# Row sums inverted before the transpose of k and q, on 32 partitions of 28 numbers

## The chip, the cores and the metric

One core of a Trainium2 chip runs the kernel. The metric is the device time of one execution in microseconds (us). Five engines work side by side: TensorE (PE; its weight loads are listed apart as PEld), VectorE (DVE), ScalarE (ACT), GpSimd (POOL) and SyncE (SP). SP does no arithmetic here, it only issues transfers (DMAs); POOL issues transfers too. Each engine takes its instructions in the order of its own queue, and an instruction that waits holds back everything behind it in that queue.

## The reference

Softcapped attention over 4 batches of 12 heads (448 rows, head size 64, float32), then a two-layer MLP with a squared ReLU on its output (1792 tokens, 768 to 2048 to 768):

```python
def _attn_ref(q, k, v, cap):
    scale = 1.0 / np.sqrt(q.shape[-1])
    scores = scale * np.matmul(q, k.transpose(0, 1, 3, 2))
    scores = cap * np.tanh(scores / cap)
    scores = scores - np.max(scores, axis=-1, keepdims=True)
    attn = np.exp(scores)
    attn = attn / (np.sum(attn, axis=-1, keepdims=True) + 1e-09)
    return np.matmul(attn, v)

def _moe_ref(x, w_in, w_out):
    h = np.maximum(x @ w_in, 0.0)
    return h * h @ w_out
```

## The kernel before

The 48 heads are taken two at a time, as 24 pairs. The loop `for n in range(NP + 1)` (lines 535 to 586) is a software pipeline with several pairs in flight; one turn of it is called a pass here. The order of the instructions on PE, ACT, DVE, POOL and SP is written out by hand (`manual_schedule`), so the order of the source lines is the order of each queue. Pass n holds:

- On PE the scores of pair n (line 366, with half scores of two pairs at line 374 in even passes), and then, for pair n-1, the products of the probabilities with v (lines 408 and 424, into `pa`) and the row sums (lines 411 and 417, into `pb`). `pa` and `pb` have one PSUM buffer each: the first value matmul of a pass (line 408) has to wait until the pair before was copied out of them, the sums by `take_sums` (line 434, `es`) and the values by `evac` (line 429, `e`).
- On ACT tanh and exp of pair n (lines 384 and 392).
- On DVE in this order: `add_p3(n-1)` (line 399), `turn_kq(n+2)` (line 359, the transpose of k and q), `invert(n-2)` (lines 441 and 442), a piece of the decoding of `w_in`, the copy in `take_sums(n-1)` (line 434), `add_p(n)` (line 396), `normalise(n-3)` (lines 457, 460, 461) and `evac(n-1)` (line 429).
- On SP: the loads of q for pair n+3 and a part of n+4 (line 321, `load_part`; a pair is four parts of 56 KB, and passes 3 to 6 load five parts), the write of the inverted sums (line 444), from pass 4 on now and then a load of raw `w_in` (line 264, 384 KB), and the two transfers that bring the sums into `cmp` (line 437).
- On POOL: the two copies of the inverted sums of pair n-3 (`spread`, line 452), the loads of v (line 346) and the loads of k (line 321).

A pair's row sums take this way: the copy at line 434 brings them into SBUF; two transfers lay them out as `cmp` (112 partitions of 8 numbers); `invert` adds 1e-9 and takes the reciprocal on DVE; SP writes them to `rd` in DRAM; POOL reads them back over 64 partitions each as `rb`; `normalise` multiplies the values by them. In pass n, `cmp` of pair n-1 is sent, pair n-2 is inverted, and pair n-3 is spread and normalised.

k and q have three raw buffers (`kqn`). A load for pair n+3 goes where pair n was, whose transpose was two passes earlier. After pass 24 the MLP follows: the products with `w_in` (line 299) and with `w_out` (line 738).

Of the kernel before, what the change touches and what calls it, by code (L numbers as in the profile page):

```python
# [10 lines left out]
F32 = mybir.dt.float32  # L11
# [5 lines left out]
ALU = mybir.AluOpType  # L17
# [171 lines left out]
def tile_softcap_attention_mlp(ctx, tc, q, k, v, cap, w_in, w_out, out):  # L189
    nc = tc.nc  # L190
    B, H, S, D = q.shape
    NT, DM = out.shape
    DFF = w_in.shape[1]
    P = 128
    NS = S // D
    NT32 = S // 32
    HS = S // 2
# [38 lines left out]
    guard = const.tile([P, 1], F32, name="guard")  # L236
# [3 lines left out]
    ep = actx.enter_context(tc.tile_pool(name="ep", bufs=2))  # L240
# [76 lines left out]
    def load_part(n, i, a, queue):  # L317
        b, j = divmod(n, NPAIR)
        h, w = divmod(a, 2)
        x = (k, q)[i][b, 2 * j + h, :, 32 * w:32 * w + 32].rearrange("(t r) e -> r t e", r=32)  # L320
        queue.dma_start(out=kqn[n % NKQ][32 * a:32 * a + 32, i], in_=x)  # L321
# [19 lines left out]
    def load_v(n):  # L341
        b, j = divmod(n, NPAIR)
        x = v[b, 2 * j:2 * j + 2].rearrange("h (t r) d -> (h t) r d", r=D)
        for i in range(2):
            r, at = (bottom, 0) if (n + i) % 2 else (top, n % 2)
            nc.gpsimd.dma_start(out=vn[n % NKV][r, at:at + NS], in_=x[i::2].rearrange("t r d -> r t d"))
# [5 lines left out]
    kqs, ps, probs, adds, pvs, es, rds = {}, {}, {}, {}, {}, {}, {}  # L352


    def turn_kq(n, parts=1):
        kqs[n] = qp.tile([P, 2 * S], F32, tag="kq", name="kq")
        src, w = kqn[n % NKQ].rearrange("p i t e -> p (i t e)"), 2 * S // parts
        for i in range(parts):
            done = nc.vector.transpose(out=kqs[n][:, i * w:(i + 1) * w], in_=src[:, i * w:(i + 1) * w])  # L359
            last.setdefault("turn", done)  # L360

    def scores(n, u):
        sc = ps_s.tile([P, 2, 512], F32, tag="s", name="sc")
        kt, qt = kqs[n][:, :S], kqs[n][:, S:]
        for h, r in enumerate((top, bottom)):
            nc.tensor.matmul(out=sc[:, h, :S], lhsT=kt[r, keys(n, h, u)], rhs=qt[r], start=True, stop=True)  # L366
        probs[n, u] = sc
# [10 lines left out]
    def tanh(n, u):  # L378
        if u in (1, 3):
            c = 2 if u == 3 and n % 2 else 4  # L380
            ps[n, u // 3] = pp.tile([P, c, S], F32, tag=f"p{c}{u}", name="p", bufs=2 if c == 4 else 1)
        at = 2 * (u in (2, 0))
        p = ps[n, int(u not in (1, 2))][:, at:at + 2]
        nc.scalar.activation(out=p, in_=probs[n, u][:, :, :S], func=ACTF.Tanh, scale=qks)  # L384
        if u:
            probs[n, u] = p
        else:
            probs[n, 0], probs[n + 1, 0] = p[:, 0], p[:, 1]

    def exp(n, i):  # L390
        p = ps.pop((n, i))
        nc.scalar.activation(out=p, in_=p, func=ACTF.Exp, scale=cap_sb)  # L392
# [5 lines left out]
    def add_p3(n):  # L398
        nc.vector.tensor_add(out=adds[n], in0=adds[n], in1=probs[n, 3])
# [13 lines left out]
    def sums(n):  # L413
        a = adds.pop(n)
        for i in range(4):
            h, c = 1 - i // 2, slice(i % 2 * HS, (i % 2 + 1) * HS)
            nc.tensor.matmul(out=pvs[n, 1][32 * i:32 * i + 32, c], lhsT=ones[:, :32], rhs=a[:, h, c],  # L417
                             start=False, stop=True, tile_position=(0, 32 * i))
# [8 lines left out]
    def evac(n):  # L427
        es[n] = ep.tile([P, S], F32, tag="e", name="e", bufs=NE)
        nc.vector.tensor_copy(out=es[n], in_=pvs.pop((n, 0)))  # L429


    def take_sums(n):
        e = ep.tile([P, S], F32, tag="es", name="es", bufs=1)
        nc.vector.tensor_copy(out=e, in_=pvs.pop((n, 1)))
        rds[n] = ep.tile([P - 16, 8], F32, tag="cmp", name="cmp", bufs=NE)
        for c in range(2):
            nc.sync.dma_start(out=rds[n][c * 56:c * 56 + 56], in_=e[32 * c:P:64, c * HS:(c + 1) * HS])

    def invert(n):
        cmp = rds[n]  # L440
        nc.vector.tensor_scalar(out=cmp, in0=cmp, scalar1=guard[:P - 16], scalar2=None, op0=ALU.add)
        nc.vector.reciprocal(out=cmp, in_=cmp)
        rd = dram.tile([2, 2, HS], F32, tag="rd", name="rd")
        nc.sync.dma_start(out=rd.rearrange("c i (o e) -> (c i o) e", e=8), in_=cmp)
        rds[n] = rd


    def spread(n):
        rd = rds[n]
        rds[n] = ep.tile([P, S], F32, tag="rb", name="rb", bufs=2)  # L450
        for h, r in enumerate((top, bottom)):
            last["dma"] = nc.gpsimd.dma_start(out=rds[n][r].rearrange("p (c q) -> p c q", c=2), in_=rd[:, 1 - h].partition_broadcast(D))  # L452
# [34 lines left out]
    def prepare_cap():  # L487

        nc.vector.tensor_scalar_mul(ncap, cap_sb, -1.0)
        nc.vector.tensor_tensor(out=ncap, in0=ncap, in1=cap_sb, op=ALU.min)  # L490
        nc.vector.tensor_scalar(out=far, in0=ncap[0:1], scalar1=-CAP_MAX, scalar2=None, op0=ALU.is_lt)

        nc.scalar.activation(out=guard, in_=ncap, func=ACTF.Exp)

    def early_work():

        halves = [(f, o) for f in range(NEARLY + NW2) for o in range(0, DM, HO)]
        raw = fetch_w(scr, *halves[0], True, 2)
        yield
        for i, (f, o) in enumerate(halves):  # L500
            while f == NEARLY and not tail:
                yield
            if o == 0:
                hi, lo = hold_win(f, *((wpool, EARLY) if f < NEARLY else (qp, LATE)))
            coming = []
            if i + 1 < len(halves):
                wanted.append((coming, halves[i + 1]))
                if tail:
                    fetch_wanted()
            yield from decode_f64(nc, scr, raw, hi[:, o:o + HO], lo[:, o:o + HO], HO, NSCR,  # L510
                                  alone=lambda: not tail)
            raw = coming and coming[0]
            if o:
                decoded.append(f)
# [6 lines left out]
    decoded, tail, wanted = [], [], []  # L521
    decoding = early_work()
    NE = 2
    AHEAD = 1, 0
    START, DEEP = 4, 3

    def decode(count):
        for _ in range(count):
            next(decoding, None)

    def unit(f, b):
        hps[b, f] = ps_s.tile([P, 2, 512], F32, tag="s", name="hps")[:, 0, :S]
        mlp1_part(b, f, 0, 3 * KDM)

    for n in range(NP + 1):
        on, prep, old = n < NP, n + 1 < NP, n > 0

        if on:
            for u in (1, 2, 3):
                scores(n, u)  # L540
            tanh(n, 1)
            tanh(n, 2)
            exp(n, 0)
            tanh(n, 3)
        if n >= 3:
            spread(n - 3)
        if prep:
            load_v(n + 1)
        if n == 0:
            prepare_cap()  # L550
        if old:
            add_p3(n - 1)
        if 0 < n < NP - 2:
            turn_kq(2 if n == 1 else n + 2)
        upto = [min(4 * (m + 4) + min(4, max(0, m + 1 - DEEP)), 4 * NP) for m in (n - 1, n)]
        for i, queue in enumerate((nc.gpsimd, nc.sync)):
            for at in range(*upto):
                load_part(at // 4, i, at % 4, queue)
        if n == 1:
            nc.vector.tensor_scalar_mul(guard, guard, 1e-9)  # L560
        if n >= 2:
            invert(n - 2)
        if n >= START:
            decode(1 if n < NP - 2 else n - NP + 4)
        if n == NP:
            unit(0, 0)
        if old:
            pv_half(n - 1)
        if on and n % 2 == 0:
            half_scores(n)  # L570
            tanh(n, 0)
        if on:
            exp(n, 1)
        if old:
            sums(n - 1)
            take_sums(n - 1)
            fetch_wanted()
            pv(n - 1)
        if on:
            add_p(n)  # L580
        if n == 1:
            turn_kq(3)
        if n >= 3:
            normalise(n - 3)
        if old:
            evac(n - 1)
# [3 lines left out]
    units = [(f, b) for f in (0, 1) for b in range(B - 1)] + [(f, B - 1) for f in (0, 1)]  # L590
    units += [(f, b) for f in range(2, NEARLY) for b in range(B)] + [(NEARLY, b) for b in AHEAD]
    for i, (f, b) in enumerate(units):
# [90 lines left out]
    for f in range(NEARLY, NF):  # L683
# [19 lines left out]
        for b in reversed(range(B)):  # L703
            if f == NEARLY and b in AHEAD:
                continue
# [5 lines left out]
    with ExitStack() as mctx:  # L711
# [132 lines left out]
        for z in range(-6, N + 1):  # L844
# [9 lines left out]
            if 0 <= z + 2 < N:  # L854
                m, i = PRODUCTS[z + 2]
                ops[m, i] = operand(raws[m, i])
            if 0 <= z < N:
                weights(z)
                m, i = PRODUCTS[z]
# [39 lines left out]
```

## Time and profile before

| | us |
|---|---|
| median of 3 runs | 616.8 (616.15 to 618.32) |
| the profiled execution | 617.65 |
| its span from first to last instruction | 616.0 |
| PE busy | 602.5 (98%) |
| DVE busy | 484.6 (79%) |
| ACT busy | 336.1 (55%) |
| POOL busy | 125.6 (20%) |

The span is what the profile shows of one execution; what lies around it is 1.65 us. A busy PE is modelled from the starts of its matmuls. Shares over the whole span mix three stages: attention (to about 171 us), the first product of the MLP (to about 371 us) and the second. In the rows below a line such as L441 is line 441 of the kernel before. Idle time stands in brackets with the one that ended it by semaphore order; where the engine named had long been done, a transfer ended it.

### The profile page before, as it was taken

The numbers are of one execution on the slowest core, as the hardware profiler recorded it, in microseconds if no ns is written. First come the engines' busy times: TensorE is split into PE (matmuls) and PEld (weight loads), VectorE is DVE, ScalarE is ACT, GpSimd is POOL, SyncE is SP. The second block draws the span as 40 slices with busy tenths as digits, with TensorE's granted clock in tenths as the row PEclk, the third lists the DMA queues.
The fourth block names the chain that finished last, engine by engine and source line by source line (L and its number), as shares of the span: only waits on it lengthen the run. The fifth ranks groups of instructions, "written<-read, shape, count | busy, mean of one in ns | idle before, by whom it ended". The sixth has DMA issues, their size and how long they took to land.

```text
span 616.0 us, 9630 instructions
## 1 busy us (share of the span) xinstructions
PE 602.5 (98%) x3412; PEld 481.5 (78%) x3412; DVE 484.6 (79%) x840; ACT 336.1 (55%) x410; POOL 125.6 (20%) x197
## 2 busy tenths in 40 slices
PE   7998999999999999999999999999999999999997
PEld 4333333333369998999999999999999999999997
DVE  2778999999889663888999999834799998666752
ACT  5998899999933232555565555535334542222220
POOL 8678877686220000000000000000000000000000
PEclk9999999999999999999999999999999999999999
DMA  9999666774335433466657787689599807666611
GB/s 133 119 164 170 146 133 141 156 150 106 92 97 168 132 118 125 160 201 208 191 175 209 245 250 246 225 243 351 146 282 294 210 2 196 165 166 176 176 38 42
DMA packets 151671, 103.90 MB, mean 169 GB/s; under 512 B 58209, under 2 KB 142433, under 8 KB 151617
## 3 DMA queue, kind: packets, MB, share of 16 engines
q1 hardware_dynamic: 142432, 86.55, 52.4%
q0 software_dynamic: 7648, 16.41, 12.1%
q8 instruction: 28, 0.46, 0.3%
q10 hardware_dynamic: 1536, 0.27, 0.3%
q14 instruction: 27, 0.21, 0.1%
HBM read 79.69 MB, written 23.42 MB: 167 GB/s over the span
## 4 chain that ended last, share of the span: by engine, by line
PE 80%; DMA 9%; DVE 4%; POOL 2%; issue 2%; ACT 1%; SPq 0%; ACTq 0%; POOLq 0%; DVEq 0%
PE hps L299 32%; PE po L738 31%; PE pa L424 7%; PE sc L366 6%; DMA kqn<-in_k_dram 4%; PE pa L408 2%; DMA a<-g_dram 2%; PE pb L417 1%; POOL kqn L321 1%; DMA g_dram<-r 1%; PE sc L374 1%; DMA vn<-in_v_dram 1%; DMA rd<-cmp 1%; DMA rb<-rd 1%; DVE s L72 1%
## 5 line engine op out<-in xcount | busy, mean ns | idle before, releaser
L299 PE MATMUL hps<-xs,kq 128*128 128x448 f32 x864 | 173.2, 362 | 0.6 <-ACT r L303 0.6
L299 PEld LDWEIGHTS hps<-xs,kq 128*128 128x128 f32 x864 | 161.9, 187 | 11.8 <-ACT r L303 1.0
L738 PE MATMUL po<-th,gl 128*128 128x384 f32 x392 | 131.8, 336 | 0.6 <-DVE gl L728 0.6
L738 PE MATMUL po<-th,gh 128*128 128x384 f32 x392 | 131.8, 336 | 0.0
L738 PE MATMUL po<-tl,gh 128*128 128x384 f32 x392 | 131.7, 336 | 0.0
L727 ACT CAST gh<-a 128x1024 fp32r<-128x1024 f32 x49 | 51.6, 1053 | 110.8 <-PE po L738 103.4
L384 ACT ACTIVATE p<-sc,qks 128x896 f32<-128x896 f32 x84 | 80.4, 996 | 11.7 <-PE sc L366 11.5
L728 DVE TENSOR_TENSOR gl<-a,gh 128x1024 fp32r<-128x1024 f32 x49 | 59.9, 1223 | 28.6 <-ACT gh L727 28.5
L392 ACT ACTIVATE p<-p,cap_sb 128x1792 f32<-128x1792 f32 (+1 forms) x48 | 76.9, 1603 | 1.5
L303 ACT ACTIVATE r<-hps 128x448 f32<-128x448 f32 x64 | 34.8, 544 | 78.5 <-PE hps L299 78.5
L738 PEld LDWEIGHTS po<-th,gl 128*128 128x128 f32 x392 | 73.7, 188 | 1.0 <-DVE gl L728 1.0
L738 PEld LDWEIGHTS po<-th,gh 128*128 128x128 f32 x392 | 73.7, 188 | 0.3 <-ACT gh L727 0.3
L738 PEld LDWEIGHTS po<-tl,gh 128*128 128x128 f32 x392 | 73.7, 188 | 0.0
L366 PE MATMUL sc<-kq 64*128 64x448 f32 x288 | 60.6, 553 | 0.5 <-DVE kq L359 0.5
L424 PE MATMUL pa<-p,vn 128*64 128x448 f32 x288 | 59.4, 548 | 0.0
L321 POOL DMA_DIRECT2D kqn<-in_k_dram x92 | 58.8, 646 | 2.0 <-DMA kqn<-in_k_dram 1.0
L299 PE MATMUL hps<-xs,whi 128*128 128x448 f32 x192 | 54.1, 363 | 0.0
L366 PEld LDWEIGHTS sc<-kq 64*128 64x128 f32 x288 | 25.8, 186 | 34.4 <-issue 18.7
L424 PEld LDWEIGHTS pa<-p,vn 128*64 128x64 f32 x288 | 18.5, 136 | 30.9 <-issue 30.5
L452 POOL DMA_DIRECT2D rb<-rd x48 | 29.1, 611 | 54.6 <-DVE e L429 10.1
L299 PEld LDWEIGHTS hps<-xs,whi 128*128 128x128 f32 x192 | 35.8, 187 | 3.6 <-issue 1.4
L751 DVE TENSOR_TENSOR osb<-s,po 128x384 f32<-128x384 f32 x27 | 14.9, 553 | 27.4 <-PE po L738 27.3
(80 smaller groups left out, 746.8 us busy)
## 6 DMA issues: line engine op xcount, KB each, us to landing
a<-g_dram SPq DMA_DIRECT2D x56, 512.0 KB
g_dram<-r SPq DMA_DIRECT2D x64, 224.0 KB
wraw<-in_moe_w_in_dram SPq DMA_DIRECT2D x32, 384.0 KB
wraw<-in_moe_w_out_dram SPq DMA_DIRECT2D x32, 384.0 KB
vn<-in_v_dram POOLq DMA_DIRECT2D x48, 112.0 KB, 4.0
rb<-rd POOLq DMA_DIRECT2D x48, 112.0 KB, 3.6
kqn<-in_q_dram SPq DMA_DIRECT2D x93, 56.0 KB
kqn<-in_k_dram POOLq DMA_DIRECT2D x92, 56.0 KB, 3.7
```

The costliest lines, as they stand in the source:

```text
L299: nc.tensor.matmul(out=ps, lhsT=w[:, c * P:(c + 1) * P], rhs=x[b, c], start=(n == 0), stop=(n == 3 * KDM - 1))
L303: nc.scalar.activation(out=r, in_=ps, func=ACTF.Relu)
L321: queue.dma_start(out=kqn[n % NKQ][32 * a:32 * a + 32, i], in_=x)
L366: nc.tensor.matmul(out=sc[:, h, :S], lhsT=kt[r, keys(n, h, u)], rhs=qt[r], start=True, stop=True)
L384: nc.scalar.activation(out=p, in_=probs[n, u][:, :, :S], func=ACTF.Tanh, scale=qks)
L392: nc.scalar.activation(out=p, in_=p, func=ACTF.Exp, scale=cap_sb)
L424: nc.tensor.matmul(out=pvs[n, 0][r], lhsT=vn[n % NKV][:, v_slot(n, h, u)], rhs=p[:, h], start=False, stop=(u == NU - 1))
L452: last["dma"] = nc.gpsimd.dma_start(out=rds[n][r].rearrange("p (c q) -> p c q", c=2), in_=rd[:, 1 - h].partition_broadcast(D))
L727: last["act"] = nc.scalar.copy(out=hi, in_=x)
L728: last["dve"] = nc.vector.tensor_sub(out=lo, in0=x, in1=f32(hi))
L738: last["mm"] = nc.tensor.matmul(out=po, lhsT=w[:, c], rhs=m[:, cols], start=(c == 0 and i == 0), stop=(c == HF - 1 and i == 2))
L751: nc.vector.tensor_tensor(out=osb, in0=x, in1=y, op=op)
```

## The change

The inversion of the row sums stands ahead of `turn_kq` and of the loads of k and q in each pass, and no longer behind them. `cmp` becomes 32 partitions of 28 numbers: the two transfers into it move 16 runs of 112 bytes each where they moved 56 runs of 32 bytes, and the write to `rd` moves 32 runs of 112 bytes where it moved 112 of 32.

```diff
 def take_sums(n):
     e = ep.tile([P, S], F32, tag="es", name="es", bufs=1)
     nc.vector.tensor_copy(out=e, in_=pvs.pop((n, 1)))
-    rds[n] = ep.tile([P - 16, 8], F32, tag="cmp", name="cmp", bufs=NE)
+    rds[n] = ep.tile([NC, HB], F32, tag="cmp", name="cmp", bufs=NE)
     for c in range(2):
-        nc.sync.dma_start(out=rds[n][c * 56:c * 56 + 56], in_=e[32 * c:P:64, c * HS:(c + 1) * HS])
+        nc.sync.dma_start(out=rds[n][c * (NC // 2):(c + 1) * (NC // 2)], in_=e[32 * c:P:64, c * HS:(c + 1) * HS])

 def invert(n):
     cmp = rds[n]
-    nc.vector.tensor_scalar(out=cmp, in0=cmp, scalar1=guard[:P - 16], scalar2=None, op0=ALU.add)
+    nc.vector.tensor_scalar(out=cmp, in0=cmp, scalar1=guard[:NC], scalar2=None, op0=ALU.add)
     nc.vector.reciprocal(out=cmp, in_=cmp)
     rd = dram.tile([2, 2, HS], F32, tag="rd", name="rd")
-    nc.sync.dma_start(out=rd.rearrange("c i (o e) -> (c i o) e", e=8), in_=cmp)
+    nc.sync.dma_start(out=rd.rearrange("c i (o e) -> (c i o) e", e=HB), in_=cmp)
     rds[n] = rd
...
 NE = 2
+HB = 28
+NC = 2 * S // HB
...
     if old:
         add_p3(n - 1)
+    if n >= 2:
+        invert(n - 2)
     if 0 < n < NP - 2:
         turn_kq(2 if n == 1 else n + 2)
     upto = [min(4 * (m + 4) + min(4, max(0, m + 1 - DEEP)), 4 * NP) for m in (n - 1, n)]
...
             load_part(at // 4, i, at % 4, queue)
     if n == 1:
         nc.vector.tensor_scalar_mul(guard, guard, 1e-9)
-    if n >= 2:
-        invert(n - 2)
     if n >= START:
         decode(1 if n < NP - 2 else n - NP + 4)
```

## Rows read from the trace of the kernel before

**Rows 1.** Stretches of the span: us, busy time by engine, granted clock, DMA share, GB/s

```profile
25.00:29.00 4.00, 4.00 (x24) 1.63 (x20) 3.79 (x7) 3.97 (x5) 0.29 (x1) 1.00 0.28 40
29.00:41.00 12.00, 12.00 (x84) 4.13 (x82) 8.82 (x16) 11.77 (x11) 10.37 (x17) 1.00 1.12 153
...
67.00:171.00 104.00, 103.99 (x692) 36.79 (x692) 98.98 (x171) 99.46 (x87) 72.32 (x112) 1.00 0.58 129
...
241.00:371.00 130.00, 130.00 (x650) 121.86 (x651) 111.80 (x267) 71.75 (x133) 0.00 (x0) 1.00 0.66 206
```

**Rows 2.** Timeline of TensorE, first value matmul of passes 4, 5 and 8: start, length

```profile
35.77 0.59 PE L408 MATMUL pa<-p,vn 64*64 64x448 f32 x2
...
44.30 0.59 PE L408 MATMUL pa<-p,vn 64*64 64x448 f32 x2 [1.42 <-ACT p L384]
...
67.01 0.59 PE L408 MATMUL pa<-p,vn 64*64 64x448 f32 x2 [1.15 <-DVE e L429]
```

**Rows 3.** Chain that ended last, first value matmul of pass 10: start, length, what

```profile
80.41 0.52 PE pa L408 x2
```

**Rows 4.** Timeline of VectorE, passes 2 to 7; in brackets idle time before and releaser

```profile
22.16 1.07 DVE L399 TENSOR_TENSOR add<-add,p 128x896 f32<-128x896 f32 x1
25.01 1.11 DVE L359 STREAM_TRANSPOSE kq<-kqn 128x896 f32<-128x896 f32 x1 [1.78 <-DMA kqn<-in_k_dram]
...
35.63 1.08 DVE L399 TENSOR_TENSOR add<-add,p 128x896 f32<-128x896 f32 x1
38.99 1.11 DVE L359 STREAM_TRANSPOSE kq<-kqn 128x896 f32<-128x896 f32 x1 [2.29 <-DMA kqn<-in_q_dram]
...
44.11 1.08 DVE L399 TENSOR_TENSOR add<-add,p 128x896 f32<-128x896 f32 x1
...
46.85 0.50 DVE L441 TENSOR_SCALAR cmp<-cmp,guard 112x8 f32<-112x8 f32 x1 [0.64 <-DMA cmp<-es]
...
57.12 0.63 DVE L457 TENSOR_TENSOR rb<-e,rb 128x448 f32<-128x448 f32 x1 [0.77 <-DMA rb<-rd]
...
64.71 0.63 DVE L457 TENSOR_TENSOR rb<-e,rb 128x448 f32<-128x448 f32 x1 [0.93 <-DMA rb<-rd]
```

**Rows 5.** Timeline of the SyncE queue, passes 2 to 4, issues merged

```profile
19.85 2.98 SPq L321 DMA_DIRECT2D kqn<-in_q_dram  x4
26.50 0.33 SPq L444 DMA_DIRECT2D rd<-cmp  x1
...
28.11 2.51 SPq L321 DMA_DIRECT2D kqn<-in_q_dram  x5
31.15 0.32 SPq L444 DMA_DIRECT2D rd<-cmp  x1
...
32.76 3.03 SPq L321 DMA_DIRECT2D kqn<-in_q_dram  x5
40.58 0.32 SPq L444 DMA_DIRECT2D rd<-cmp  x1
40.95 0.43 SPq L264 DMA_DIRECT2D wraw<-in_moe_w_in_dram  x1
41.43 1.08 SPq L437 DMA_DIRECT2D cmp<-es  x2
```

**Rows 6.** Timeline of GpSimd, pass 3: the copies of the inverted sums

```profile
28.71 1.21 POOL L452 DMA_DIRECT2D rb<-rd  x2 [3.85 <-DMA rd<-cmp]
```

**Rows 7.** Chain that ended last: two transfers of the sums

```profile
27.56 1.63 DMA cmp<-es
...
31.15 4.68 DMA rd<-cmp
```

**Rows 8.** All instructions by line: mean ns of one, idle before

```profile
L441 DVE TENSOR_SCALAR cmp<-cmp,guard 112x8 f32<-112x8 f32 x24 | 6.2, 258 | 1.7 <-DMA cmp<-es 1.7
...
L442 DVE RECIPROCAL cmp<-cmp 112x8 f32<-112x8 f32 x24 | 4.9, 203 | 0.8
...
L483 DVE RECIPROCAL qks<-cap_sb 128x1 f32<-128x1 f32 x1 | 0.2, 163 | 0.3 <-DMA cap_sb<-in_cap_dram 0.3
```

## Prediction

> **What bounds the kernel now.** I read the stretches first, because shares over the whole span mix three stages. From 67 us to the end of attention PE stands still for 0.01 us of 104, and in the first product of the MLP for nothing; the granted clock is 1.00, the higher of the two levels, 2.4 GHz [rows 1]. What the change does to a pass after 67 us is therefore hidden behind PE, as long as DVE keeps up: DVE has 5.02 us to spare in those 104 us, 0.32 us for each of their 15.5 passes of 6.70 us [rows 1 to 3].
>
> Before 67 us PE is not the bound. The timeline of PE shows where passes begin: from pass 4 at 35.77 to pass 8 at 67.01 they take 31.24 us, 7.81 us each [rows 2]. Two passes of a full PE take 80.41 - 67.01 = 13.40 us [rows 2, 3], so four need 26.80. The difference, 4.44 us, is all that a change in this stage can give. PE waits there for buffers that DVE empties late, and the timeline of DVE says why DVE is late: 2.29 us at the transpose of pass 4, 0.64 us for `cmp` in pass 5, 0.77 and 0.93 us for `rb` in passes 6 and 7 [rows 4]; a fifth wait, 0.48 us for `rb` in pass 5, I leave out. Behind these waits stand transfers. The DMA engines are busy beyond one queue's worth from 29 to 41 us (1.12), yet nearly idle from 25 to 29 (0.28) [rows 1]: POOL waits 3.85 us there for the inverted sums of pair 0 [rows 6], and with it all loads of v and k behind that instruction.
>
> **The change part by part.** *The inversion moves ahead of the transpose.* In pass 2 the transpose waits 1.78 us for k and takes 1.11 us, and the write of `rd` goes out at 26.50 [rows 4, 5]. Put behind the addition that ends at 22.16 + 1.07 = 23.2, the inversion waits only for `cmp`, which I put at 23.6; it takes some 0.5 us, so `rd` leaves at 24.1, 2.4 us earlier, and POOL starts at 26.3 where it started at 28.71 [rows 6]. Loads of v and k follow 2.4 us earlier, into the hole from 25 to 29. The 2.29 us at the transpose of pass 4 have q as their releaser in the profile [rows 4], but k, which lies behind `rb` in POOL's queue, is as late. With k 2.4 us earlier and q landing in time (next part) they go: the addition of pass 4 ends at 36.7, the inversion at 37.4, and the transpose follows there and not at 38.99, 1.6 us earlier. DVE reaches the addition of pass 5 at some 42.2 and not 44.11 [rows 4].
>
> *SP's queue is turned round, and this gives most of that back.* Before, SP issued `cmp` first, then the q loads, and then waited for the next inversion: at 41.43 `cmp`, at 32.76 the five q loads of pass 4, at 40.58 `rd` [rows 5]. The loads were issued while SP waited. Now they stand behind `rd`, and `cmp` of the next pair stands behind them. In pass 2 four loads move from 19.85 to some 24.4, in pass 3 five move from 28.11 to some 30.5 [rows 5]. Their data are wanted one pass later (at some 30.1 and 37.4), 3 to 4 us after the last is issued, so I cost the loads themselves at nothing; if that cover fails, the transpose waits for the rest. What costs is `cmp`. With nothing in front a transfer of the sums takes 1.63 us; behind five q loads it takes 4.68 [rows 7]. The first was a transfer into `cmp`, the second a write to `rd`; the nearest rows there are.
>
> This makes a closed ring of waits in each pass: `rd` is issued (0.32 us), five q loads (2.51 to 3.03, taken as 2.65), two transfers into `cmp` (1.08) [rows 5], they land (call it x, in place of 1.63 to 4.68), the inversion runs (0.53) and the next `rd` is issued. The sum is 4.58 + x. DVE's own way from `rd` to that copy of sums (transpose 1.11, a piece of decoding, a copy) is shorter than the q loads. At x = 2.12 the ring takes 6.70 us, the period of a full PE; at x = 3.23 it takes 7.81, the period before; above that the change loses.
>
> Pass by pass: in pass 5 `cmp` lies behind five q loads and 384 KB of raw `w_in`. Before, only `w_in` was close ahead of it: issued from 41.43, it landed at 46.8 [rows 4, 5]. The bytes queued ahead of it since 32.76 are the same in both, so I put its landing at 46.3, while the inversion wants it at 43.2. DVE stands 3.1 us, and with the transpose then still to do, all but 0.2 us of the lead is gone. From there POOL has no work until `rd` of this pass lands, so SP's transfers find the engines free: in passes 6 and 7 I take x = 2.5, and the waits of 0.77 and 0.93 us for `rb` [rows 4] fall away, since `rd` leaves before the transpose (1.11 us). Lead 0.7 us after pass 6, 1.2 after pass 7. That is 30.0 us for the four passes, 7.5 each, a mean x of 2.9. From pass 7 on only four parts are loaded, some 0.5 us less, so the ring needs 4.1 + x and stays below 6.70 up to x = 2.6; the engines are at 0.58 there [rows 1].
>
> A rule of the Trainium skill bears on this. The rows show 1.63 us with nothing ahead and 4.68 us behind five loads [rows 7]. "DMA: Bandwidth & Descriptors", section "Queues, rings and completion order", says that each DMA engine consumes a queue's descriptors in ring order and that a semaphore update lands only after the earlier writes of that engine; by that, `cmp` always pays for the loads now ahead of it, in an idle stage too, and the sum would be that of the third rival below, 619.5. The two rows agree with the order; whether the loads ahead take long enough is x.
>
> *Fewer and longer runs.* 16 runs in place of 56, 32 in place of 112. Bounds: nothing, and the 1.63 us of a whole small transfer [rows 7]. Both stay one small transfer, so I take 0.1 us, inside x.
>
> *Longer instructions on DVE.* The reciprocal took 203 ns on 8 numbers a partition and 163 on one [rows 8]: 5.7 ns a number, so 20 more add 0.11 us. Bounds: nothing, and 203 x 28/8, 0.51 us more. The addition of 1e-9 (258 ns [rows 8]) I bound the same way, by nothing and by 0.65 us more; the rows don't part its start from its numbers, the reciprocal's slope would give it 0.11, and I take 0.02. Together 0.13 us a pass (0.22 with that slope), under the 0.32 us that DVE has to spare, which is what hides it. "VectorE: DVE Perf Modes", section "First, the fixed hardware budget", gives the reciprocal a repeat count of 8 on its divider; at that page's 0.96 GHz this is 8.3 ns a number and an estimate of 0.17 us a pass, still under the spare time.
>
> **Sum.** Profiled time 617.65 (span 616.0 and 1.65 around it), less 1.2: 616.4. The median of the runs is 616.8, 0.85 below the profiled execution, so I expect 615.6. The lead reaches the end because PE hardly stops after 67 us [rows 1].
>
> **The rivals.** *Full gain* (x at 2.1 or less from pass 4 on): DVE stays ahead and PE never waits: up to 4.44 us, half to all of it likely, about 3.4, so 613.4. For it: 1.63 us with free engines, and the hole filled. Against it: 1.12 of DMA share until pass 5 [rows 1].
> *Nothing* (x near 3.2): the waits at `rb` become waits at `cmp` of the same length; 616.8. It is also what comes if the transpose was late by q and not by k.
> *Slower by the ring* (x = 3.9): `cmp` stays behind the q loads, the inversion blocks DVE ahead of the transpose, 8.48 us a pass, +2.7 over four passes: 619.5. It decides from x = 3.23; for it stands 4.68, against it that POOL goes idle while SP loads.
> *Slower by DVE*: at the upper bounds (0.51 + 0.65 - 0.32 = 0.84 us over 15.5 passes) +13; with the reciprocal's alone 0.19 x 15.5, +2.9: 619.7.
>
> **How the numbers follow.** Forecast 0.45 (its own range 614.3 to 617), full gain 0.22, nothing 0.17, slower by the ring 0.12, slower by DVE 0.04. A measurement tells about 0.3% from no change, 1.85 us: below 614.95 is faster, above 618.65 slower. Of the forecast 0.14 lies below, 0.29 within, 0.02 above. Faster 0.14 + 0.22 = 0.36; same 0.29 + 0.17 = 0.46; slower 0.02 + 0.12 + 0.04 = 0.18. The range leaves out the best of the full gain and the worse half of the slower cases: 612.8 to 618.6.
>
> **What would show it.** Right: POOL's first copy of sums near 26.3 and not 28.71; the transpose of pass 4 without its 2.29 us; a wait of 2 to 3 us at line 441 in pass 5; no waits at line 457 in passes 6 and 7; pass 8 on PE near 65.8 and not 67.01; the reciprocal near 0.32 us. Wrong: waits at line 441 in every pass, or a transpose that waits for q in pass 3 or 4, or PE with gaps after 67 us.

## The result and the profile after

| | median | range | runs |
|---|---|---|---|
| before | 617.22 us | 616.15 to 618.76 | 6 |
| after | 622.18 us | 620.93 to 623.29 | 6 |

The ratio is 1.0078, with a 95% interval of 1.0065 to 1.0092: slower by 0.8%, where 615.6 us and no loss had been forecast, and above the range. The profiled execution of after took 622.77 us with a span of 621.2, that of before 617.65 and 616.0: 5.1 us, and the question is where on the way from pass 2 to the end they were lost.

The timeline of TensorE in the kernel after gives the account: the first value matmul of passes 5 to 8, 18 and 24 (start, length, idle before it and releaser).

```profile
43.34 0.59 PE L408 MATMUL pa<-p,vn 64*64 64x448 f32 x2
...
53.94 1.01 PE L408 MATMUL pa<-p,vn 64*64 64x448 f32 x2 [4.24 <-DVE e L429]
...
63.24 0.59 PE L408 MATMUL pa<-p,vn 64*64 64x448 f32 x2
...
69.53 0.59 PE L408 MATMUL pa<-p,vn 64*64 64x448 f32 x2
...
138.73 0.59 PE L408 MATMUL pa<-p,vn 64*64 64x448 f32 x2 [1.77 <-DVE e L429]
...
180.43 0.59 PE L408 MATMUL pa<-p,vn 64*64 64x448 f32 x2
```

The same of before, passes 6, 7, 9, 18 and 24 (passes 4, 5 and 8 stand in [rows 2]):

```profile
51.96 0.59 PE L408 MATMUL pa<-p,vn 64*64 64x448 f32 x2 [1.26 <-DVE e L429]
...
59.46 0.59 PE L408 MATMUL pa<-p,vn 64*64 64x448 f32 x2 [0.39 <-issue]
...
74.05 0.59 PE L408 MATMUL pa<-p,vn 64*64 64x448 f32 x2
...
133.70 0.59 PE L408 MATMUL pa<-p,vn 64*64 64x448 f32 x2
...
175.05 0.59 PE L408 MATMUL pa<-p,vn 64*64 64x448 f32 x2
```

After is 0.96 us ahead in pass 5 (43.34 for 44.30). It is 1.98 us behind at pass 6 and 3.78 at pass 7, and gets 1.26 back in pass 7 (2.52 behind at pass 8, 69.53 for 67.01). At pass 24 it is 5.38 us behind, near the 5.2 by which the spans differ. So there are three losses: 2.9 us in pass 5, 1.8 in pass 6, and another 2.9 in passes 8 to 23, where PE had been thought safe.

The timeline of VectorE of the kernel after, passes 4 to 7, beside [rows 4].

```profile
37.66 0.23 DVE L441 TENSOR_SCALAR cmp<-cmp,guard 32x28 f32<-32x28 f32 x1 [0.75 <-DMA cmp<-es]
37.92 0.32 DVE L442 RECIPROCAL cmp<-cmp 32x28 f32<-32x28 f32 x1
38.29 1.11 DVE L359 STREAM_TRANSPOSE kq<-kqn 128x896 f32<-128x896 f32 x1
...
42.98 1.08 DVE L399 TENSOR_TENSOR add<-add,p 128x896 f32<-128x896 f32 x1
48.47 0.23 DVE L441 TENSOR_SCALAR cmp<-cmp,guard 32x28 f32<-32x28 f32 x1 [4.41 <-DMA cmp<-es]
...
55.13 0.23 DVE L441 TENSOR_SCALAR cmp<-cmp,guard 32x28 f32<-32x28 f32 x1 [0.25 <-DMA cmp<-es]
...
59.72 0.62 DVE L457 TENSOR_TENSOR rb<-e,rb 128x448 f32<-128x448 f32 x1
...
66.63 0.62 DVE L457 TENSOR_TENSOR rb<-e,rb 128x448 f32<-128x448 f32 x1
```

The reader is to see that the waits of [rows 4] are gone (the transpose of pass 4 at 38.29 and not 38.99, nothing at line 457). In their place stand waits for `cmp`: 0.75 us in pass 4, 0.25 in pass 6, and one of 4.41 us in pass 5. The cause of the long one is in the timeline of SyncE's queue, beside [rows 5].

```profile
24.43 0.34 SPq L444 DMA_DIRECT2D rd<-cmp  x1
...
38.26 0.33 SPq L444 DMA_DIRECT2D rd<-cmp  x1
38.63 3.71 SPq L321 DMA_DIRECT2D kqn<-in_q_dram  x5
42.38 0.48 SPq L264 DMA_DIRECT2D wraw<-in_moe_w_in_dram  x1
42.91 1.08 SPq L437 DMA_DIRECT2D cmp<-es  x2
49.08 0.33 SPq L444 DMA_DIRECT2D rd<-cmp  x1
```

The order is `rd`, five q loads, the first raw `w_in` load (384 KB), `cmp`. The trace also holds the semaphore updates of each transfer; the last one says when it has landed:

```
          transfer       issued   landed
before    w_in            40.95    45.90
before    cmp, second     42.00    46.73
after     q, fifth        41.86    43.96
after     w_in            42.38    48.07
after     cmp, second     43.48    48.38
```

All five q loads had landed by 43.96. `cmp` lands behind `w_in`, right ahead of it in both kernels: 4.73 us after its issue in before and 4.90 in after. (That it waits for `w_in` is shown below, where that load is moved.) What differs is the issue, 1.48 us later although DVE was ahead, because five q loads, which take 3.71 us to issue, now stand in front of it; and DVE wants it at 44.06, ahead of the transpose, and no longer behind it.

More views show the second and third loss. The stretches from 52 to 60 us of the kernel after (us, busy time of PE, PEld, DVE, ACT, POOL, granted clock, DMA share, GB/s):

```profile
52.00:54.00 2.00, 0.06 (x4) 0.07 (x5) 1.93 (x5) 2.00 (x2) 2.00 (x4) 0.50 0.72 150
54.00:56.00 2.00, 2.00 (x12) 0.74 (x16) 1.66 (x4) 0.09 (x1) 2.00 (x4) 0.50 0.80 212
56.00:58.00 2.00, 2.00 (x16) 0.20 (x8) 1.12 (x2) 0.71 (x1) 1.48 (x3) 0.50 1.12 220
58.00:60.00 2.00, 2.00 (x14) 0.78 (x12) 1.82 (x3) 1.97 (x2) 0.00 (x0) 0.81 1.45 135
```

While PE stands for 4.24 us the granted clock falls from 1.00 (2.4 GHz) to 0.50 (1.2 GHz), and pass 6 is computed at the lower level: its first matmul takes 1.01 us and not 0.59, and the pass 9.30 us (53.94 to 63.24) where 7.04 do at the full clock (pass 8 of before, 67.01 to 74.05).

The stretches of [rows 1] in the kernel after:

```profile
25.00:29.00 4.00, 4.00 (x28) 1.66 (x22) 2.70 (x4) 3.97 (x5) 2.05 (x4) 1.00 0.55 98
...
67.00:171.00 104.00, 101.57 (x670) 36.17 (x670) 99.88 (x166) 97.60 (x86) 71.80 (x110) 1.00 0.62 127
```

The hole from 25 to 29 us is filled, as foreseen: DMA share 0.55 for 0.28. From 67 us on PE stands 2.43 us where it stood 0.01, and DVE is busy 0.90 us longer though it has fewer instructions in the stretch (166 for 171).

Most of the third loss falls in one pass. After is 3.15 us behind when pass 17 begins (130.56 for 127.41) and 5.03 when pass 18 does (138.73 for 133.70): 1.88 of the 2.9 us. VectorE waits there once more for `cmp`:

```profile
132.56 0.37 DVE L441 TENSOR_SCALAR cmp<-cmp,guard 32x28 f32<-32x28 f32 x1 [1.10 <-DMA cmp<-es]
```

This `cmp` was issued at 129.00, behind four q loads, and landed 3.43 us later, at 132.43.

### The profile page after: what moved, and what is told of

Its sections match the earlier page's. It is cut to its first block, busy times and chain, and to the rows that moved or that the text cites. A ratio compares the mean times of both kernels' runs of the same rounds, so it can differ in the third digit from the quotient of the medians.

```text
span 621.2 us, 9607 instructions
## 1 busy us (share of the span) xinstructions
PE 604.2 (97%) x3412; PEld 481.4 (77%) x3412; DVE 489.4 (79%) x840; ACT 336.2 (54%) x410; POOL 125.2 (20%) x197
## 4 chain that ended last, share of the span: by engine, by line
PE 72%; DVE 10%; DMA 8%; ACT 4%; issue 3%; SPq 2%; POOL 1%; DVEq 0%; POOLq 0%; ACTq 0%
PE hps L299 37%; PE po L740 31%; DMA cmp<-es 4%; ACT p L384 2%; DVE kq L359 2%; DVE add L396 2%; ACT p L392 2%; PE pa L424 2%; DMA g_dram<-r 1%; DVE add L399 1%; DVE rb L457 1%; DVE es L434 1%; DMA kqn<-in_q_dram 1%; PE sc L366 1%; PE pa L408 1%
```

## The experiments

Two questions. Is it the layout (28 numbers on 32 partitions) or the place? And if it is the place: is it the order on SyncE's queue, or the order on VectorE, which the change moves together? Each ratio is to the kernel before on the same chip.

**The order alone.** The kernel after with the old layout:

```diff
-    HB = 28
+    HB = 8
```

> Only the order is changed; cmp stays 112 partitions of 8. If the loss comes from SP's turned queue (cmp behind the q loads), nearly all of it is here: 620 to 623 us, a wait of 3 us or more at line 441 in pass 5, PE idle for 3 us or more before pass 6 and a granted clock well under 1 after it. If it comes from the longer DVE instructions, this kernel stands within 1 us of the kernel before (616 to 618), with line 442 back at 203 ns.

Measured: 623.15 us, ratio 1.0099 (1.0073 to 1.0124). Pass 5 of its VectorE timeline:

```profile
47.99 0.23 DVE L441 TENSOR_SCALAR cmp<-cmp,guard 112x8 f32<-112x8 f32 x1 [3.79 <-DMA cmp<-es]
```

The place alone makes as much of a loss as the change, or more; the runs show no part of the layout in it.

**The layout alone.** The kernel after with the inversion back behind the loads:

```diff
-        if n >= 2:
-            invert(n - 2)
         if 0 < n < NP - 2:
             turn_kq(2 if n == 1 else n + 2)
...
             nc.vector.tensor_scalar_mul(guard, guard, 1e-9)
+        if n >= 2:
+            invert(n - 2)
```

> Only the layout is changed; the inversion stays behind the transpose and the loads. By the SP queue: 616 to 618 us, no wait at line 441 longer than 1 us, although line 442 takes 316 ns here too. By the longer DVE instructions: at least half of the loss, 619.5 us or more, with TensorE late by 2 us or more between passes 8 and 24.

Measured: 617.17 us, ratio 0.9996 (0.9978 to 1.0013). Fewer and longer runs, and longer instructions, together change nothing that can be measured.

**The order on SyncE alone.** The kernel before with the inversion behind the transpose, as before, but ahead of the loads: VectorE's order stays, SyncE's turns round.

```diff
             turn_kq(2 if n == 1 else n + 2)
+        if n >= 2:
+            invert(n - 2)
         upto = [min(4 * (m + 4) + min(4, max(0, m + 1 - DEEP)), 4 * NP) for m in (n - 1, n)]
...
-        if n >= 2:
-            invert(n - 2)
```

> The kernel before (112 partitions of 8), with the inversion moved only past the loads: DVE still transposes first, SP writes rd ahead of the q loads. If SP's ring alone makes the loss, 620 to 623 us with waits of 2 us or more at line 441 in pass 5. If the early place on DVE is needed for it, 616 to 618.5: the transpose gives cmp 1.1 us more to land.

It was run again on another chip:

> e6 (only SP's order turned) once more for a second profile, since the one at hand is of its fastest execution (618.3 against a median of 621.0). By the ring of waits, a slower execution shows 7 us or more of waits at line 441 (the first profile shows 7.2), and its loss lies in passes 5 to 8. If it shows no more of them than the first, what separates the executions is not cmp.

Measured: 621.0 us, ratio 1.0055 (1.0034 to 1.0076), and 621.93, ratio 1.0060 (1.0033 to 1.0087). The profile of the second shows in VectorE's timeline

```profile
50.25 0.23 DVE L441 TENSOR_SCALAR cmp<-cmp,guard 112x8 f32<-112x8 f32 x1 [3.70 <-DMA cmp<-es]
```

in pass 5, and PE is 2.38 us behind before at pass 8. It loses another 1.90 us up to pass 24, with waits of 0.65, 1.09 and 0.65 us for `cmp` (at 85.10, 119.41 and 133.31), although VectorE has its old order there. The profile of the first, an execution of 618.31 us, has 1.87 us in pass 5 and further waits of 0.94 to 1.38 in passes 3 to 7; it loses 0.81 us between passes 8 and 24. The turned queue alone costs some 0.6%. The two profiled executions differ in how long that wait of pass 5 gets; two don't show that it is the rule.

**The order on VectorE alone.** The kernel after with the inversion split: its two instructions ahead of the transpose, the write of `rd` behind the loads as before.

```diff
         nc.vector.reciprocal(out=cmp, in_=cmp)
+
+    def send(n):
+        cmp = rds[n]
         rd = dram.tile([2, 2, HS], F32, tag="rd", name="rd")
...
             nc.vector.tensor_scalar_mul(guard, guard, 1e-9)
+        if n >= 2:
+            send(n - 2)
```

> The two DVE instructions stand early, as after the change, but SP issues the write to rd at its place before the change, behind the q loads, so cmp again has no fresh q loads ahead of it. By the SP queue: the pass 5 wait at line 441 is under 2 us, PE idle before pass 6 under 2 us, the clock stays near 1.00, and the time is 614 to 617.5 us. By the early place on DVE alone (DVE blocked ahead of the transpose): 620 us or more.

> e3 once more for a second profile, since the one at hand is of its fastest execution (617.0 against a median of 620.3). If waits at line 441 make the slower executions, this profile shows more than the 1.9 us of them that the first shows; if DVE's longer work makes them, it shows DVE without idle time and late by the same 0.2 us in each pass.

And the same with the old layout (`HB = 8`):

> As e3 (DVE inverts early, SP writes rd at its place before the change), but with cmp as 112 partitions of 8, so that DVE has 0.11 us less to do in a pass. If e3's 620.3 comes from longer DVE instructions on a DVE that waits for cmp in their place, this one falls to 616 to 618 us. If it comes from the early place alone, where DVE waits for cmp with the transpose behind it, it stays at 619.5 to 621.

Measured: 620.26 us, ratio 1.0042 (1.0024 to 1.0060), and on another chip 618.57, ratio 1.0012 (0.9998 to 1.0026); with 8 numbers 619.46, ratio 1.0030 (1.0013 to 1.0048). The gain that was expected did not come. The early passes do gain (in the traces PE is ahead of before at pass 8 by 2.58, 0.46 and 1.32 us), and passes 8 to 23 lose 1.70, 2.28 and 3.12 us again. The layout is not why, since 8 numbers lose as much as 28. Nor are waits at line 441: the second profile, of a slower execution, has 1.6 us of them, the first 1.9. (The first profile is of an execution of 617.0 us, the fastest of nine; no trace shows one near their median.)

VectorE's timeline says where time goes. The addition of a pass, what follows it, and the next copy or piece of decoding, in before:

```profile
93.11 1.08 DVE L399 TENSOR_TENSOR add<-add,p 128x896 f32<-128x896 f32 x1
94.11 1.10 DVE L359 STREAM_TRANSPOSE kq<-kqn 128x896 f32<-128x896 f32 x1
95.14 0.19 DVE L441 TENSOR_SCALAR cmp<-cmp,guard 112x8 f32<-112x8 f32 x1
95.36 0.20 DVE L442 RECIPROCAL cmp<-cmp 112x8 f32<-112x8 f32 x1
95.48 0.51 DVE L55 TENSOR_TENSOR t<-s,whi 128x384 f32<-128x384 f32 x1
```

and in the old layout with the early place (the last experiment):

```profile
72.53 1.08 DVE L399 TENSOR_TENSOR add<-add,p 128x896 f32<-128x896 f32 x1
73.53 0.35 DVE L441 TENSOR_SCALAR cmp<-cmp,guard 112x8 f32<-112x8 f32 x1
73.91 0.20 DVE L442 RECIPROCAL cmp<-cmp 112x8 f32<-112x8 f32 x1
74.28 1.11 DVE L359 STREAM_TRANSPOSE kq<-kqn 128x896 f32<-128x896 f32 x1 [0.17 <-DMA kqn<-in_q_dram]
```

In before what follows the reciprocal starts 0.12 us after it, ahead of its end; the transpose starts 0.37 us after it. The chain of that experiment shows what lies between:

```profile
73.91 0.03 DVE cmp L442
73.94 0.05 issue
73.99 0.05 DVEq L359
74.04 0.05 issue
...
74.24 0.05 issue
74.28 1.11 DVE kq L359
```

These are the transpose's own waits, three instructions of VectorE's queue (at 73.99, 74.09 and 74.19), some 0.1 us each with the step to the next. What they wait for is there, since each takes 0.05 us (the bracket above names q by semaphore order alone), but they still have to go by. Behind the addition of 1.08 us they are covered, since the transpose of before starts ahead of its end; behind a short reciprocal they are not. From the start of the addition to the start of what follows the group, as a median over those passes from 60 to 172 us in which nothing waits for `cmp` (10 to 14 in each trace):

| kernel | inversion | numbers | us |
|---|---|---|---|
| before | behind the transpose | 8 | 2.37 |
| layout alone | behind | 28 | 2.49 |
| order on SyncE alone, two traces | behind | 8 | 2.50, 2.40 |
| order alone | ahead | 8 | 2.67 |
| order on VectorE, 8 numbers | ahead | 8 | 2.74 |
| order on VectorE, two traces | ahead | 28 | 2.67, 2.69 |
| after | ahead | 28 | 2.69 |
| first `w_in` load behind `cmp`, two traces, below | ahead | 28 | 2.60, 2.60 |
| early to pass 6 only, the two kernels below | behind from pass 7 | 8 | 2.38, 2.46 |

The early place costs VectorE 0.30 to 0.37 us a pass at 8 numbers. In the rows above 0.25 of it is the step to the transpose (0.37 for 0.12), and the rest a longer addition of 1e-9 (0.35 for 0.19), whose cause no run shows. At 28 numbers, where the longer reciprocal covers a part of the waits, the place costs 0.11 to 0.20 us beside the layout alone, and the longer instructions 0.12.

How much of the loss of passes 8 to 23 this makes, single traces don't tell. With both orders as before in those passes, the layout alone loses 1.62 us there, and the last three kernels below 0.48, 0.74 and 0.17.

**The first `w_in` load behind `cmp`.** The kernel after, with pass 4's piece of decoding, which issues that load, moved:

```diff
-        if n >= START:
+        if n > START:
             decode(1 if n < NP - 2 else n - NP + 4)
...
             take_sums(n - 1)
+            if n == START:
+                decode(1)
```

> The changed kernel, but the first load of raw w_in in pass 4 is issued behind cmp and not ahead of it. If the 384 KB ahead of cmp make the stall of pass 5 and this the drop of the clock: the wait at line 441 in pass 5 falls from 4.4 to 1 to 2 us, the clock stays near 1.00, pass 8 begins 2 us or more earlier, and the time is 618 to 620 us. If the q loads alone make it: the wait stays over 3 us and the time at 621 to 623.

> e4 (the changed kernel with the first w_in load behind cmp) once more for a second profile, its first being of its fastest execution (619.4 against 620.7). By the theory the wait at line 441 in pass 5 stays under 2.2 us, and the granted clock in 49 to 60 us stays above 0.9; waits in passes 6 and 7 remain, since w_in now lies ahead of the next write of rd.

Measured: 620.73 us, ratio 1.0058 (1.0038 to 1.0078), and 620.21, ratio 1.0048 (1.0031 to 1.0065). The wait of pass 5 is gone and the granted clock stays at 1.00, but the first trace has in passes 6 and 7

```profile
52.88 0.23 DVE L441 TENSOR_SCALAR cmp<-cmp,guard 32x28 f32<-32x28 f32 x1 [2.16 <-DMA cmp<-es]
...
60.80 0.44 DVE L441 TENSOR_SCALAR cmp<-cmp,guard 32x28 f32<-32x28 f32 x1 [1.13 <-DMA cmp<-es]
```

The landings explain both. In pass 5 `cmp` lies behind five q loads alone and lands 2.13 us after its issue (42.10 to 44.23). In pass 6 the q loads go out from 45.30 on, while the load is still under way (42.66 to 47.65); they take 5.0 to 5.8 us, and `cmp` behind them 4.23 (48.56 to 52.79). The load moves the wait on and keeps part of it: 1.2 to 1.9 us of the 4.8 came back (0.58 and 0.48% beside 0.78; the first interval overlaps that of after).

**Early in two passes only.** The kernel before, with the whole inversion early in passes 2 and 3, to keep the filled hole and no ring:

```diff
+        if n in (2, 3):
+            invert(n - 2)
         if 0 < n < NP - 2:
...
-        if n >= 2:
+        if n > 3:
             invert(n - 2)
```

> The kernel before, with the inversion early only in passes 2 and 3, where the DMA engines stand idle while POOL waits for the first sums; from pass 4 on everything as before. By the ring of waits, the lead of 1 us that the changed kernel has at pass 5 is kept, since cmp of pass 5 has no q loads of its own pass ahead of it: 614 to 616.5 us, no wait over 1 us at line 441 in pass 5. If the lead is always lost to DVE or to transfers that come due later: 616.5 to 618.

Measured: 617.98 us, ratio 1.0005 (0.9991 to 1.0020). PE is 1.46 us ahead at pass 8 of its trace and 0.98 at pass 24; the median shows nothing of it. `cmp` still makes VectorE wait 1.45 us in pass 5 (at 46.22), where no wait over 1 us had been expected.

**Early on VectorE up to pass 6, SyncE as before.** The kernel before with the split of above:

```diff
+        if 2 <= n <= 6:
+            invert(n - 2)
         if 0 < n < NP - 2:
...
-        if n >= 2:
+        if n > 6:
             invert(n - 2)
+        if n >= 2:
+            send(n - 2)
```

> The kernel before (112 partitions of 8), with DVE inverting early in passes 2 to 6 only and SP writing rd at its place before the change in all passes. If e5 loses in the passes after 8, where DVE has nothing to spare, and gains before them, this one keeps the gain: 615 to 617 us, TensorE 1 us or more ahead at pass 8 and still 0.7 us ahead at pass 24. If the early place gains nothing in the passes up to 6 either: 617 to 618.5.

Measured: 617.15 us, ratio 0.9998 (0.9982 to 1.0014). From pass 8 to 24 PE loses 0.74 us here and not the 3.12 of the kernel with the early place in all passes, 8 numbers too, whose ratio was 1.0030 (1.0013 to 1.0048): without the early place in the full passes that loss mostly goes. It rests on one trace of each and on intervals that just touch. A wait of 1.55 us for `cmp` in pass 5 is left.

**The same, and the first `w_in` load behind `cmp`.** Both edits together on the kernel before:

> e8 (early on DVE in passes 2 to 6, SP's order as before the change) and the first w_in load of pass 4 behind cmp, as in e4. If the 1.55 us that e8 still waits at line 441 in pass 5 are the w_in load ahead of cmp, they go, TensorE is 2 us or more ahead at pass 8, and the time is 614.5 to 616.5 us, the fastest of all. If the load then delays what comes after it by as much (rd or the q loads of pass 5): 616.5 to 618, as e8.

Measured: 616.69 us, ratio 0.9986 (0.9970 to 1.0003), the fastest of all, though not clearly faster than before. `cmp` makes no wait in pass 5; PE is 2.25 us ahead at pass 8 and 2.08 at pass 24 of its trace, which has a span of 614.3 us. Its VectorE timeline shows what is left in passes 5 and 6: waits of 1.29 and 1.38 us for `rb` (at 47.90 and 56.09).

## Why the prediction was wrong

**What bounds the kernel: half right.** The early stage does wait for transfers, and its ceiling stands (80.41 is a time of the chain and 67.01 one of the timeline; with the timeline's 80.34 it is 4.6 and not 4.44 us). "Hidden behind PE, as long as DVE keeps up" was right too, but the room was misread: of the 5.02 us in which DVE stands in [rows 1], more than half is DVE waiting for PE, ACT or a transfer. Waits of VectorE from 67 to 180 us, before (us in total, times, longest):

```profile
DVE es L434 <- PE pb L417: 1.3, 2, 1.0
DVE add L396 <- ACT p L392: 0.9, 4, 0.4
DVE add L399 <- ACT p L392: 0.7, 2, 0.3
DVE rb L457 <- DMA rb<-rd: 0.2, 1, 0.2
```

and after:

```profile
DVE cmp L441 <- DMA cmp<-es: 1.9, 3, 1.1
```

Such a wait is room only as long as DVE is ahead, so the full 0.32 us a pass was not safe to spend; this is argued, no run takes these waits away alone. In the terms of the sum, "less 1.2" at pass 8 came out as 2.52 more, and "PE hardly stops after 67 us" as another 2.9.

**The inversion moves ahead: right on the transfers, one price left out.** `rd` leaves at 24.43 (24.1 forecast), POOL's first copy of sums starts at 27.26 (26.3; 28.71 before):

```profile
27.26 1.21 POOL L452 DMA_DIRECT2D rb<-rd  x2 [1.95 <-DMA rd<-cmp]
```

The transpose of pass 4 starts at 38.29 without its 2.29 us (37.4 forecast; 0.75 us go to a wait for `cmp`), and no transpose waits for q. What has no place in the sum is that the swap itself costs VectorE time in every pass, 0.20 us in the kernel after (2.69 for 2.49): the part counted the instructions moved and not the waits of the transpose that come out from under the addition. With the 0.12 us of the longer instructions that is the whole of the 0.32 us. It makes VectorE late, and the kernel that drops the early place from pass 7 on loses 0.74 us where its fellow loses 3.12; but in the kernel after most of the loss of passes 8 to 23 comes with a wait for `cmp`, so SyncE's queue has its part there too.

**SP's queue is turned round: the ring is right in kind, one term failed.** In pass 6 `cmp` lands 2.41 us after the second issue (52.62 to 55.03), in pass 7 2.99 (59.40 to 62.39), and DVE waits there 0.25 us and not at all; the 2.5 taken for these passes is near. (That pass 7 shows no wait is partly luck, since pass 6 took 9.30 us at the lower clock; and in the trace of the order alone the transfer took 3.78 us and the wait of pass 6 was 1.47.) The step that failed is the landing in pass 5: "the bytes queued ahead of it since 32.76 are the same in both, so I put its landing at 46.3". It landed at 48.38. It was not the bytes queued over ten microseconds that counted but its own issue and what was still under way ahead of it then: `w_in` takes 4.95 us in before and 5.69 in after, `cmp` comes in behind it, and both are issued some 1.5 us later, behind five q loads that took 3.71 us to issue and not 2.65. The wait was 4.41 us and not 3.1, the lead of 0.2 us a lag of 1.98. With the load out of the way the wait of that pass is gone, which shows the cause of that wait; that it comes back in the next two passes shows that the ring is short of room until `w_in` is in.

The ring was also to stay below a full PE from pass 7 on, up to x = 2.6. Its fixed part was put too high: from `rd` at 49.08 to `rd` at 55.74 it takes 6.66 us with x = 2.41, which leaves 4.25 and not 4.58 (the 1.08 us hold the second issue, and x is counted from its start). With one load less the bound for x is then near 2.9. As a median x is 2.31 there, but the `cmp` of passes 8, 14 and 16 took 3.54, 3.02 and 3.43 us, and VectorE waited for each of them in the pass after: 0.49, 0.35 and 1.10 us. So the ring binds now and then in passes that the prediction held to be safe.

The Trainium skill's rule that the prediction weighed ("DMA: Bandwidth & Descriptors", "Queues, rings and completion order") agrees with these landings: `cmp` was in 0.31 us after `w_in` (48.38 for 48.07), and in the trace of the moved load 1.15 us after the last q load (44.23 for 43.08). Whole transfers do not always land in order, though: in pass 7 of after `cmp` was in 0.14 us before the last q load ahead of it (62.39 for 62.53). The prediction put the rule to the q loads, behind which alone `cmp` took 2.13 us, 0.50 more than with nothing ahead; in pass 5 it was the 384 KB that cost.

**TensorE's clock** had no part in the prediction. In the profiled execution pass 6 is 2.3 us longer at the lower level. It is not needed for the loss, though: the second trace of SyncE's order alone has a stand of 3.39 us at that place with the granted clock at 1.00 after it, and is 2.38 us behind at pass 8 all the same. The mean granted clock of each execution bears on what it is worth in the medians. Of 94 executions of before on four chips 19 have 0.997 or less, and they are 1.5 to 2.5 us longer, as medians by chip, than the others. Of the six of after four have 0.993 to 0.995 (621.70 to 623.29 us), but the two at 0.999 and 1.000 still take 620.93 and 622.40. So the lower clock goes with a part of the loss and not with most of it; whether it makes that part, or only marks the executions with the longer stands, no run shows.

**Longer instructions and longer runs: right.** The reciprocal was put near 0.32 us; by line, all 24:

```profile
L442 DVE RECIPROCAL cmp<-cmp 32x28 f32<-32x28 f32 x24 | 7.6, 316 | 0.8
...
L441 DVE TENSOR_SCALAR cmp<-cmp,guard 32x28 f32<-32x28 f32 x24 | 7.0, 290 | 7.9 <-DMA cmp<-es 7.8
```

**The rivals.** "Slower by the ring" was the case that came, at 619.5 with a chance of 0.12. Its mechanism measures 0.55 and 0.60% alone, some 3.5 us where 2.7 had been put; its place was wrong, one long wait in pass 5 and not x = 3.9 in four passes. The order on VectorE adds 0.1 to 0.4%. Together that is 0.7 to 1.0%, against 0.78 for the kernel after and 0.99 for the order alone; the intervals are too wide to say whether the two simply add. Also open: why the split inversion with 28 numbers gave 1.0042 on one chip and 1.0012 on another. A lag between passes 8 and 24 in one trace is worth no more than some 1.6 us: the layout alone shows that much in its profile, with a median equal to before. So the split of the third loss between the two orders stays open.

## What to carry to other kernels

A step that is moved takes its transfers with it: write down the new order of the issuing queue, and ask of each small transfer in it what large one is still under way when it is issued, and who stops for it. The order of instructions on an engine and the order of issues on a queue can be moved apart, and each should be priced alone. Idle time of an engine that is spent waiting for the bound is not room, and the waits of an instruction cost nothing only as long as they stand behind a long one.

## What was not expected of the hardware

- Waits that are long satisfied still take some 0.1 us each on VectorE's queue: 0.37 us from the start of a reciprocal to that of a transpose behind such waits, whether the reciprocal took 0.20 us (order on VectorE, 8 numbers, 73.91) or 0.32 (after, 37.92; 0.30 as the median of its passes from 60 us on). To an instruction without them it is 0.12 us behind one of 0.20 (before) and 0.24 behind one of 0.32 (layout alone).
- The length of one stand of PE did not say whether the granted clock falls: with 4.24 us (after), 3.75 (order alone) and 1.98 (second trace of the split inversion) it went to 0.50; after 3.39 (second trace of SyncE's order) it stayed at 1.00.
- In pass 5, 1.8 KB behind 384 KB landed 4.9 us after its issue (after), and 2.1 us behind five loads of 56 KB alone (first `w_in` load behind `cmp`).
